# A transformer kernel whose first MLP matmul goes from groups of four to groups of six column blocks

## The chip, the core and the metric

The kernel runs on one core of a Trainium2 chip. The metric is the device time of one execution in microseconds (us). Before the change the median of 8 runs is 940.08 us (937.43 to 942.26).

The engines are PE (TensorE: matmuls), PEld (its weight loads), ACT (ScalarE: exp and gelu, which also empties the PSUM banks of scores and of the first MLP matmul), DVE (VectorE: LayerNorm, copies out of PSUM, residuals), POOL (GpSimd: masks, powers, bias) and SP, whose queue issues nearly all DMAs. PSUM, into which PE writes, has eight banks of 512 fp32 columns.

## What is computed

Two layers, the same weights in both, over x of 2048 tokens by 576. Each layer is sliding-window attention (32 heads of 18, window 256, causal) and an MLP of width 4608, both behind a LayerNorm and added to x. The MLP's input goes through LayerNorm twice, which the kernel does in one step:

```python
x = x + _A_ref(_layernorm(x, axis=-1), A_wqkv, A_wo)    # softmax attention, then @ wo
x = x + _B_ref(_layernorm(x, axis=-1), B_w1, B_b1, B_w2, B_b2)

def _B_ref(x, w1, b1, w2, b2):
    y = _layernorm(x, axis=-1)
    h = _gelu(jnp.einsum("bsd,df->bsf", y, w1) + b1)
    return jnp.einsum("bsf,fd->bsd", h, w2) + b2
```

## The kernel before

**Chunks.** The tokens are cut into chunks of 512 (four tiles of 128); two layers make eight chunks, k = 0 to 7. For each chunk the kernel projects q, k and v (`qkv`, matmul at L674), computes scores (`scores`, L744), exp on ACT (L753), masks on POOL (L774), the product with v (`pv`, L791), then in `tail` the output projection (L674 again, with `wo_sb`), the residual (L825), the LayerNorm and a DMA transpose into `xnTm`.

**MLP.** It goes in two halves of 18 column blocks of 128 (of 36). `G_part(k, hf)` makes a half of the first matmul: h = gelu(xn @ w1 + b1), transposed, 512 tokens wide, one PSUM bank a block. `mm2(k, hf)` multiplies it by w2 (L912) into banks 4, 5 and 6: for each of four tiles and two column halves three runs of six matmuls.

**A group in `G_part`.** The 576 rows of w1 are four full slabs of 128 and a remainder of 64. A group of up to four column blocks starts with `rest` (L872): one matmul of 64 rows for each block, in pairs that sit in the upper and the lower half of the array (`tile_position`), which opens the blocks' banks. Then come four full-array matmuls a block (L884) and, for each block, a gelu on ACT (L887). `rest` is one step of the plan: it takes the banks of all its blocks before its first matmul. Groups don't cross a multiple of four, so that a half of 18 goes 4, 4, 4, 4, 2 or 2, 4, 4, 4, 4. Banks come from `MM1`, 0 to 6; bank 7 belongs to `pv`; scores take two pairs out of banks 0 to 5 for each task; projections and `mm2` use 4 to 6.

**w1.** It is not kept on chip: every chunk loads it anew, by `w1_load`, in nine pieces of 512 columns into `NB1 = 4` slots of `w1_sb`. A piece is three DMAs on SP: one of 512 KB for the four slabs and two of 32 KB for the remainder. A slot's next load is asked for when its last block is through. Three pieces are asked for during chunk 0's attention ("aq3", "aq5", "aq7": when the third, fifth and seventh head group is through, counted from 0) and one when the first tile of `xnTm` has landed.

**What sets the order.** Nothing is written in execution order. `add` records steps with an engine, a cost, a latency and a priority; `Plan.schedule` lists them: at each step it takes the one that can start first by its own costs, and among those the lowest priority number, and gives it PSUM banks. `PL.nudge` shifts the priority of a stage (names such as "ea2", first half of chunk 2's scores; "gb1", second half of chunk 1's first matmul; "ma1", `mm2` of the first half; "q3.0", projection of a tile; "t3", `tail`). Scores and `G_part` keep one order among themselves (`fifo="pa"`). A step marked `hold` (`rest`) goes ahead of other PE work that would start up to 0.3 us before it. Each engine then runs its list in order and waits on semaphores where an operand or a bank is not ready.

The diff touches the constants and the table of `build_kernel` (from L409), `w1_load` (L642), `G_part` (L848), `mm2` (L898) and the first loads in the loop over chunks (L994 to L1031).

Of the kernel before, what the change touches and what calls it, by code (L numbers as in the profile page):

```python
# [6 lines left out]
BF16 = mybir.dt.bfloat16  # L7
ACT = mybir.ActivationFunctionType
ALU = mybir.AluOpType
P = 128  # L10
# [398 lines left out]
def build_kernel(nc, A_x, A_wqkv, A_wo, B_x, B_w1, B_b1, B_w2, B_b2, out):  # L409
# [8 lines left out]
    NF = F // P  # L418
    NFH = NF // 2
# [4 lines left out]
    KS = 6  # L424
    VS = 10
    PS = 3
    NB1 = 4
    NXN = 4
    NQN = 6
    WB = 6  # L430
# [8 lines left out]
    add = PL.add  # L439


    PL.nudge = {"le0+": 14.98, "q1.0": -6.62, "q1.1": 0.41, "q1.3": 0.01, "ln2": 3.13, "t0": 4.51, "ga0": -13.62, "eb1": -1.75, "q2.0": 0.19,
                "gb0": 2.91, "ln3": -4.64, "ea2": -5.93, "ma1": 3.04, "q3.0": -15.52, "q3.1": -5.81, "q3.3": -1.41, "t2": -3.4, "gb1": -2.88,
                "gb1+": -3.15, "ea3": -21.36, "mb1": -13.4, "ga2": -20.18, "ma2": 38.73, "q4.1": 1.36, "q4.2": -3.02, "q4.3": -7.11, "t3": 1.4,
                "gb2": -13.15, "gb2+": 8.35, "ln5": 1.81, "ea4": -8.49, "mb2": 6.23, "eb4": 15.12, "ma3": 29.41, "q5.0": 25.69, "q5.3": 6.9,
                "t4": 2.63, "mb3": 0.61, "eb5": 3.2, "ma4": 22.07, "ma4+": -0.97, "q6.0": 10.19, "q6.1": 9.59, "q6.3": -1.52, "t5": 0.86,
                "gb4": -2.59, "ma5": -0.01, "q7.0": -0.08, "q7.3": 14.52, "t6": 19.58, "gb5": -10.21, "mb5": 35.03, "ga6": -2.82, "ma6": 11.09,
                "t7": 1.59}

    def sb(name, shape, dtype):  # L450
        return nc.alloc_sbuf_tensor(name, shape, dtype)

    x_res = sb("x_res", [P, NT, D], FP32)
    w1_sb = sb("w1_sb", [P, NB1, 2304], BF16)
    w2_sb = sb("w2_sb", [P, NFH, D], BF16)
    wqkv = sb("wqkv", [P, KD, 3 * D], BF16)
    wo_sb = sb("wo_sb", [P, KD, D], BF16)
# [42 lines left out]
    def mm_cost(n):  # L500
        return max(n / 2400.0, 0.026) + (0.003 if n > 64 else 0.0)
# [23 lines left out]
    def dma(q, out_, in_, reads=(), writes=(), cls="w", ring=8, **kw):  # L525
        n = 2 if cls != "xr" else 4
        for s in out_.shape:
            n *= s
        kw.setdefault("lat", 2.0)
        kw.setdefault("move", n / 330e3)  # L530
        kw.setdefault("desc", n // 1152)
        add(q, lambda e: e.dma_start(out_, in_), reads=reads, writes=writes, dma=cls, ring=ring, **kw)
# [101 lines left out]

    w1n = [0]

    def straddles(group):


        return group * 4 < NFH < group * 4 + 4  # L640

    def w1_load(prio, reads=()):  # L642
        B = w1n[0]
        if B >= NK * 9:
            return
        w1n[0] += 1
        sl = B % NB1
        bb = B % 9
        cols = slice(bb * 512, (bb + 1) * 512)
        dma("sp", w1_sb[:, sl, 0:2048].rearrange("p (c f) -> p c f", c=4), B_w1[0:512, cols].rearrange("(c p) f -> p c f", p=P),  # L650
            reads=reads, writes=[f"w1a{sl}"], cls="w1", cost=0.55, lat=2.0, move=1.45, desc=512, prio=prio)
        src = B_w1[512:576, cols].rearrange("p (a b f) -> p b a f", a=2, b=2)
        if not straddles(bb):
            src = B_w1[512:576, cols].rearrange("p (b a f) -> p b a f", a=2, b=2)
        for b in range(2):
            dma("sp", w1_sb[64 * b:64 * b + 64, sl, 2048:2304].rearrange("p (a f) -> p a f", a=2), src[:, b],
                writes=[f"w1b{sl}_{b}"], cls="w1", cost=0.6, lat=1.4, move=0.22 if straddles(bb) else 0.18, desc=128 if straddles(bb) else 64, prio=prio)

    def w2_load(hf, prio, gate=False):
        for b in range(NFH // WB):  # L660
# [187 lines left out]
    def G_part(k, hf, prio):  # L848
        l, t0, nt = CH[k]
        n = nt * 128  # L850
        table("gelu", prio)
        TXm = [f"xm{k % 2}_{i}" for i in range(nt)]
        f1 = (hf + 1) * NFH
        f = hf * NFH
        while f < f1:
            n4 = min(4 - f % 4, f1 - f)
            fs = range(f, f + n4)
            f += n4
            sl = (k * 9 + fs[0] // 4) % NB1
            bks = [Bank(MM1) for _ in fs]  # L860
            rd = [f"w1a{sl}", f"w1b{sl}_0", f"w1b{sl}_1"] + TXm

            def rest(e, fs=fs, sl=sl, bks=bks):

                ins = None
                at = [(ff % 4, bk) for ff, bk in zip(fs, bks)]
                if not straddles(fs[0] // 4):
                    at = [at[i] for i in (0, 2, 1, 3)]
                for n2, (i, bk) in enumerate(at):
                    b = n2 % 2  # L870
                    col = 2048 + (i // 2 if straddles(fs[0] // 4) else i % 2) * 128
                    ins = e.matmul(bank(bk)[:, 0:n], w1_sb[64 * b:64 * b + 64, sl, col:col + 128], xnTm[64 * b:64 * b + 64, k % 2, 4, 0:n],  # L872
                                   start=True, stop=False, tile_position=(64 * b, 0))
                return ins
            add("pe", rest, reads=rd, writes=bks, cost=mm_cost(n) * (n4 // 2) + 0.21, hold=True, prio=prio, alloc=bks, fifo="pa",
                after=[f"h{ff - hf * NFH}" for ff in fs])
            for ff, bk in zip(fs, bks):
                fl = ff - hf * NFH

                def fn(e, ff=ff, sl=sl, bk=bk):  # L880
                    ins = None
                    for c in range(4):
                        col = c * 512 + (ff % 4) * 128
                        ins = e.matmul(bank(bk)[:, 0:n], w1_sb[:, sl, col:col + 128], xnTm[:, k % 2, c, 0:n], start=False, stop=(c == 3))  # L884
                    return ins
                add("pe", fn, reads=rd, writes=[bk], cost=mm_cost(n) * 4, prio=prio, lat=0.22, fifo="pa")
                add("act", lambda e, ff=ff, fl=fl, bk=bk: e.activation(hT[:, fl, 0:n], bank(bk)[:, 0:n], ACT.Gelu_apprx_tanh,  # L887
                                                                      bias=b1col[:, ff:ff + 1]),
                    reads=[bk, "b1"], writes=[f"h{fl}"] + (xin_under(fl) if k == 0 and hf == 0 else []), cost=0.145 + n * 0.00087, lat=0.17, fifo="act", prio=prio)
            if fs[-1] % 4 == 3:  # L890
                w1_load(prio - 2)
            if hf == 0 and fs[0] // 4 < nt:
                t = t0 + fs[0] // 4
                add("pool", lambda e, t=t: e.tensor_tensor(x_res[:, t, :], x_res[:, t, :], b2bc[:, :], ALU.add),  # L894
                    reads=["b2", f"h{fs[0]}"], writes=X(t), cost=1.4, prio=prio)
        table("exp", prio)

    def mm2(k, hf, prio):  # L898
        l, t0, nt = CH[k]
        for i in range(nt):  # L900
            t = t0 + i
            fin = hf == 1 and l == NL - 1
            if fin:
                osl = xn_ctr[0] % NXN
                xn_ctr[0] += 1
            for hh in range(2):
                b = Bank(FILL)
                for f0 in range(0, NFH, 6):
                    def fn(e, hh=hh, b=b, f0=f0, i=i):
                        ins = None  # L910
                        for fl in range(f0, f0 + 6):
                            ins = e.matmul(bank(b)[:, 0:HB], hT[:, fl, i * 128:(i + 1) * 128], w2_sb[:, fl, hh * HB:(hh + 1) * HB],  # L912
                                           start=(fl == 0), stop=(fl == NFH - 1))
                        return ins
                    add("pe", fn, reads=[f"h{fl}" for fl in range(f0, f0 + 6)] + [f"w2s{f0 // WB}"], writes=[b],
                        cost=6 * mm_cost(HB), lat=0.22, prio=prio + 0.05 * i, alloc=((b,) if f0 == 0 else ()))
                resid(t, hh, b, prio, outp=(osl if fin else None))
            if fin:
                dma("sp", out_dram[t * P:(t + 1) * P, :], xn[:, osl, 0:D], reads=[f"xn{osl}", f"xd{osl}"], cls="o", ring=4, cost=0.5,
                    prio=prio)  # L920
            elif hf == 1:
                ln_stats(t, prio)
# [57 lines left out]
    for k in range(NK + 1):  # L980
# [23 lines left out]
        if not last:  # L1004
            PL.stage = f"eb{k}"
            E(k, range(CUT.get(k, 4), 8), b + 1.5)
            PL.stage = f"le{k}"
            if k == 0:
                w1_load(-1, ["aq5"])
                w1_load(-1, ["aq7"])  # L1010
            if k == 1:
                for n, kk in enumerate(later):
                    x_load(CH[kk][1], CH[kk][2], [], b + 2)
                    if kk > 2:
                        stats0(kk)
# [72 lines left out]
```

## Time and profile before

| | |
|---|---|
| median of 8 runs | 940.08 us |
| the profiled execution | 940.01 us |
| its span, first to last instruction | 937.9 us |
| granted PE clock, mean of the span | 0.996 |
| first MLP matmul, full array (L884) | 1152 matmuls, 263.8 us busy |
| its remainder, `rest` (L872) | 288 matmuls, 45.0 us busy |
| second MLP matmul (L912) | 2304 matmuls, 314.8 us busy |
| projections (L674) | 1280 matmuls, 179.6 us busy |
| exp (L753) and gelu (L887) on ACT | 348.7 and 196.8 us busy |
| w1 to landing (512 KB; 32 KB) | 4.4 us; 4.1 us (medians) |
| w2 to landing (864 KB) | 6.5 us |

A profile is one execution. In it a line such as `782.13 3.63 PE L884 MATMUL ... x16` gives the start and the length of a run of equal instructions, both in us, then engine, line, operation, tiles and number; a bracket at the end gives the idle time before it and who ended it. Matmuls overlap in the pipeline, so a run ends after the next one has started; the time from start to start is what a run costs PE.

### The profile page before, as it was taken

The page shows a single profiled execution, that of the slowest core. Times are in us where ns is not written, and L with a number is a line of the kernel's source. Part 1 is how long each engine was busy: PE and PEld are TensorE (multiplying, and loading weights), DVE is VectorE, ACT ScalarE, POOL GpSimd, SP SyncE. Part 2 cuts the span into 40 slices and gives each one's busy share as a digit, 9 for nine tenths or more (in the row PEclk, how much of TensorE's full clock was granted, in tenths as well). Part 3 has the DMA queues.
Part 4 walks back from the last instruction along what each step waited for, and adds up shares of the span by engine and source line. Part 5 has one row for each costly group of instructions (what it writes and reads, how often), then busy time and mean ns, then how long its engine had stood idle before and what let it go on. Part 6 is the DMA issues. An engine that isn't in the chain of part 4 may idle for free. (4 is left out here: it accounts for less than half of the span.)

```text
span 937.9 us, 22541 instructions
## 1 busy us (share of the span) xinstructions
PE 906.8 (97%) x9382; PEld 559.9 (60%) x9382; DVE 317.1 (34%) x796; ACT 593.7 (63%) x717; POOL 373.1 (40%) x507
## 2 busy tenths in 40 slices
PE   8888999999999999999999999999999999999998
PEld 6555465664755747566564647656464674656556
DVE  6646311571225512164222614234111630223001
ACT  3777677656764777565666766657777377871541
POOL 3757444354522635143340743316452263601100
PEclk9989999999999999999999999999999999999999
DMA  9996838736089340984549360693608716094440
GB/s 217 166 203 105 193 101 227 166 58 214 2 162 239 122 109 3 221 178 79 175 75 253 67 190 26 110 257 75 194 25 226 146 48 210 13 260 118 147 139 26
DMA packets 230932, 130.06 MB, mean 139 GB/s; under 512 B 140848, under 2 KB 228656, under 8 KB 230832
## 3 DMA queue, kind: packets, MB, share of 16 engines
q1 hardware_dynamic: 221520, 120.95, 53.9%
q0 software_dynamic: 6880, 5.03, 3.3%
q10 hardware_dynamic: 2432, 2.65, 0.9%
q8 instruction: 74, 1.21, 0.6%
q14 instruction: 26, 0.21, 0.1%
HBM read 91.87 MB, written 2.36 MB: 100 GB/s over the span
## 5 line engine op out<-in xcount | busy, mean ns | idle before, releaser
L753 ACT ACTIVATE pT<-ps 128x1024 bf16<-128x1024 f32 (+2 forms) x384 | 348.7, 972 | 145.7 <-PE ps L744 144.1
L774 POOL TENSOR_SCALAR_AFFINE_SELECT pT<-pT 128x512 bf16<-128x512 bf16 (+1 forms) x368 | 281.8, 789 | 269.1 <-ACT pT L753 258.1
L912 PE MATMUL ps<-w_sb,hT 128*128 128x288 bf16 x2304 | 314.8, 286 | 1.9 <-DMA w_sb<-in_B_w_dram 1.1
L887 ACT ACTIVATE hT<-ps,b1col 128x512 bf16<-128x512 f32 x288 | 196.8, 687 | 165.4 <-PE ps L884 165.2
L884 PE MATMUL ps<-xnTm,w_sb 128*128 128x512 bf16 x1152 | 263.8, 380 | 0.0
L912 PEld LDWEIGHTS ps<-w_sb,hT 128*128 128x128 bf16 x2304 | 211.6, 97 | 74.0 <-issue 18.0
L884 PEld LDWEIGHTS ps<-xnTm,w_sb 128*128 128x128 bf16 x1152 | 106.0, 98 | 142.3 <-issue 26.9
L825 DVE TENSOR_TENSOR x_res<-ps,x_res 128x288 f32<-128x288 f32 x160 | 71.0, 449 | 252.1 <-PE ps L912 205.4
L674 PE MATMUL ps<-wqkv,xnTa 128*128 128x288 bf16 x960 | 135.4, 289 | 7.8 <-DVE qn L709 3.2
L674 PEld LDWEIGHTS ps<-wqkv,xnTa 128*128 128x128 bf16 x960 | 87.7, 98 | 41.8 <-DVE qn L709 7.0
L791 PEld LDWEIGHTS ps<-vA,pT 128*128 128x128 bf16 x2880 | 94.4, 96 | 27.4 <-POOL pT L774 9.2
L791 PE MATMUL ps<-vA,pT 128*128 128x20 bf16 x2880 | 100.3, 172 | 4.5 <-DVE attq L806 2.7
L894 POOL TENSOR_TENSOR x_res<-x_res,b2bc 128x576 f32<-128x576 f32 x32 | 44.8, 1400 | 89.4 <-ACT hT L887 89.4
L709 DVE CAST qn<-ps 128x288 bf16<-128x288 f32 x120 | 54.1, 455 | 68.2 <-PE ps L674 53.0
L744 PE MATMUL ps<-qT,kT 32*128 32x384 bf16 (+2 forms) x1216 | 64.5, 278 | 6.5 <-ACT pT L753 1.9
L599 POOL TENSOR_SCALAR vtmp<-mv_all 128x1 f32<-128x1 f32 (+1 forms) x43 | 9.0, 210 | 138.3 <-DVE mv_all L590 136.8
L801 DVE RECIPROCAL rinv<-ps 128x16 f32<-128x16 f32 x64 | 16.3, 254 | 115.4 <-PE ps L791 114.9
L696 DVE CAST vA<-ps 128x288 bf16<-128x288 f32 x64 | 28.9, 456 | 77.6 <-PE ps L674 77.5
L588 DVE BATCH_NORM_STATS2 st_all<-x_res 128x6 f32<-128x288 f32 x104 | 44.8, 447 | 9.6 <-DMA x_res<-in_A_x_dram 8.5
L872 PE MATMUL ps<-xnTm,w_sb 64*128 64x512 bf16 x288 | 45.0, 381 | 1.9 <-DMA xnTm<-xn 1.1
L674 PE MATMUL ps<-wo_sb,attT 128*128 128x288 bf16 x320 | 44.2, 286 | 2.0 <-DVE x_res L825 1.1
L611 DVE TENSOR_SCALAR xn<-x_res,mv_all,rstd 128x576 bf16<-128x576 f32 x52 | 35.8, 688 | 21.4 <-DMA xnTm<-xn 16.4
(39 smaller groups left out, 268.9 us busy)
## 6 DMA issues: line engine op xcount, KB each, us to landing
w_sb<-in_B_w_dram SPq DMA_DIRECT2D x48, 864.0 KB, 6.5
w_sb<-in_B_w_dram SPq DMA_DIRECT2D x72, 512.0 KB, 4.4
w_sb<-in_B_w_dram SPq DMA_DIRECT2D x144, 32.0 KB, 4.1
x_res<-in_A_x_dram POOLq DMA_DIRECT2D x4, 1152.0 KB, 10.0
out_dram<-xn SPq DMA_DIRECT2D x16, 144.0 KB, 1.9
wqkv<-in_A_wqkv_dram ACTq DMA_DIRECT2D x3, 576.0 KB, 7.1
hT<-in_A_x_dram SPq DMA_DIRECT2D x2, 576.0 KB, 5.9
wo_sb<-in_A_wo_dram ACTq DMA_DIRECT2D x1, 576.0 KB, 6.6
```

The costliest lines, as they stand in the source:

```text
L588: add("dve", lambda e, i=i, s=s: e.bn_stats(st_all[:, t, i, :], s[:, t, i * HB:(i + 1) * HB]), reads=res, writes=[f"st{t}_{i}"], cost=0.37 ...
L674: ins = e.matmul(bank(bs[o])[:, 0:HB], lhs(c), rhs(c, o * HB), start=(c == 0), stop=(c == KD - 1))
L709: add("dve", lambda e, b=bs[o], dst=dst: e.tensor_copy(dst, bank(b)[:, 0:HB].rearrange("p (h d) -> p h d", d=DH)), reads=[bs[o]], writes=[ ...
L744: ins = e.matmul(two(bs[j // 2])[:, j % 2, col:col + nq * 128], k_of(T0 + so)[0][32 * j:32 * j + 32, g, :], qs[32 * j:32 * j + 32, g, qo * ...
L753: add("act", lambda e, h2=h2: e.activation(pT[:, sl, 2 * h2:2 * h2 + 2, lo:hi], two(bs[h2])[:, :, lo:hi], ACT.Exp, scale=SCALE), reads=[bs ...
L774: add("pool", lambda e, ap=ap, pat=pat, sgn=sgn, kind=kind: e.affine_select(ap, ap, pattern=pat, compare_op=(ALU.is_ge if kind == "d" else ...
L791: ins = e.matmul(bank(B_O)[:, o:o + VW], pT[:, sl, j, col + qi * 128:col + (qi + 1) * 128], vA[:, (T0 + so) % VS, 4 * g + j, :], start=(fi ...
L825: add("dve", lambda e: e.tensor_tensor(x_res[:, t, sl], bank(b)[:, 0:HB], x_res[:, t, sl], ALU.add), reads=[b], writes=[f"x{t}h{hh}"], cos ...
L872: ins = e.matmul(bank(bk)[:, 0:n], w1_sb[64 * b:64 * b + 64, sl, col:col + 128], xnTm[64 * b:64 * b + 64, k % 2, 4, 0:n], start=True, stop ...
L884: ins = e.matmul(bank(bk)[:, 0:n], w1_sb[:, sl, col:col + 128], xnTm[:, k % 2, c, 0:n], start=False, stop=(c == 3))
L887: add("act", lambda e, ff=ff, fl=fl, bk=bk: e.activation(hT[:, fl, 0:n], bank(bk)[:, 0:n], ACT.Gelu_apprx_tanh, bias=b1col[:, ff:ff + 1]), ...
L912: ins = e.matmul(bank(b)[:, 0:HB], hT[:, fl, i * 128:(i + 1) * 128], w2_sb[:, fl, hh * HB:(hh + 1) * HB], start=(fl == 0), stop=(fl == NFH ...
```

## The change

`G_part` now takes a half in three groups of six blocks, and w1 comes in six pieces of 768 columns a chunk, one a group, into three slots (18 DMAs a chunk instead of 27, 768 KB and twice 48 KB a piece; the bytes are the same in total). Two pieces are asked for during chunk 0's attention ("aq3", "aq6") and the third with the first tile of `xnTm`. The step that adds b2 to x stays with every fourth block. In `mm2` the first run of six of every output but a half's first one now waits for all 18 blocks of h. The table of priorities is another one; the shifts that it holds are not repeated here.

```diff
-    NB1 = 4
+    NB1 = 3
+    GS = 6
+    GW = GS * 128
+    NGR = NF // GS
+    PAT = (6, 6, 6)
...
-    PL.nudge = {"le0+": 14.98, "q1.0": -6.62, "q1.1": 0.41, "q1.3": 0.01, "ln2": 3.13, "t0": 4.51, "ga0": -13.62, "eb1": -1.75, "q2.0": 0.19,
...
+    PL.nudge = {"ea0": -16.73, "q1.0": -5.72, "q1.1": -31.53, "q1.3": 1.29, "t0": 1.55, "ea1": -1.2, "eb1": 1.29, "ma0": 1.68, "q2.0": 33.42,
...
-    w1_sb = sb("w1_sb", [P, NB1, 2304], BF16)
+    w1_sb = sb("w1_sb", [P, NB1, 4 * GW + GW // 2], BF16)
...
-        dma("sp", w1_sb[:, sl, 0:2048].rearrange("p (c f) -> p c f", c=4), B_w1[0:512, cols].rearrange("(c p) f -> p c f", p=P),
-            reads=reads, writes=[f"w1a{sl}"], cls="w1", cost=0.55, lat=2.0, move=1.45, desc=512, prio=prio)
+        dma("sp", w1_sb[:, sl, 0:4 * GW].rearrange("p (c f) -> p c f", c=4), B_w1[0:512, cols].rearrange("(c p) f -> p c f", p=P),
+            reads=reads, writes=[f"w1a{sl}"], cls="w1", cost=0.55, lat=2.0, move=2.15, desc=512, prio=prio)
...
-        while f < f1:
-            n4 = min(4 - f % 4, f1 - f)
+        for n4 in PAT:
             fs = range(f, f + n4)
             f += n4
-            sl = (k * 9 + fs[0] // 4) % NB1
+            sls = [(k * NGR + ff // GS) % NB1 for ff in fs]
             bks = [Bank(MM1) for _ in fs]
...
-            if fs[-1] % 4 == 3:
-                w1_load(prio - 2)
...
+                if ff % GS == GS - 1:
+                    w1_load(prio - 2)
...
-                    add("pe", fn, reads=[f"h{fl}" for fl in range(f0, f0 + 6)] + [f"w2s{f0 // WB}"], writes=[b],
+                    add("pe", fn, reads=[f"h{fl}" for fl in range(f0, f0 + 6 if f0 or i + hh == 0 else NFH)] + [f"w2s{f0 // WB}"], writes=[b],
...
-                w1_load(-1, ["aq5"])
-                w1_load(-1, ["aq7"])
+                w1_load(-1, ["aq6"])
```

## The prediction

> **What bounds the kernel now.** I read the engine table first, then the stretches, then the waits of TensorE (PE), then the timeline around the changed code.
>
> Of the page:
>
> ```profile
> span 937.9 us, 22541 instructions
> PE 906.8 (97%) x9382; PEld 559.9 (60%) x9382; DVE 317.1 (34%) x796; ACT 593.7 (63%) x717; POOL 373.1 (40%) x507
> ```
>
> PE is busy 906.8 of 937.9 us; 31.1 us are left. Busy time by stretches (columns: stretch, length, busy time of PE, PEld, DVE, ACT, POOL, then granted clock, DMA):
>
> ```profile
> 0.00:50.00 50.00, 42.97 (x481) 29.91 (x482) 32.02 (x89) 27.88 (x41) 28.16 (x51) 1.00 1.26 200
> 50.00:100.00 50.00, 42.00 (x631) 27.54 (x629) 26.90 (x68) 35.61 (x44) 33.80 (x50) 0.93 0.80 149
> 300.00:450.00 150.00, 149.45 (x1612) 93.13 (x1605) 54.70 (x139) 99.82 (x120) 64.62 (x85) 1.00 0.53 123
> ```
>
> Half of what is left, 15.0 us, lies in the first 100 us, before any MLP. Later PE is all but full (149.45 of 150). So a saving must come out of PE's own time, and any new wait is paid in full. Who made PE wait, in total:
>
> ```profile
> PE ps L744 <- ACT pT L753: 3.4, 11, 0.5
> PE ps L674 <- DVE qn L709: 3.2, 7, 0.9
> PE ps L674 <- DMA xnTa<-xn: 3.1, 1, 3.1
> ...
> PE ps L912 <- DMA w_sb<-in_B_w_dram: 1.1, 1, 1.1
> ```
>
> Weights made PE wait once, 1.1 us; no wait is above 3.4 us. The changed place, PE alone:
>
> ```profile
> 782.13 3.63 PE L884 MATMUL ps<-xnTm,w_sb 128*128 128x512 bf16 x16
> 785.69 0.60 PE L872 MATMUL ps<-xnTm,w_sb 64*128 64x512 bf16 x4
> 786.23 3.63 PE L884 MATMUL ps<-xnTm,w_sb 128*128 128x512 bf16 x16
> ```
>
> Matmuls overlap, so I count from start to start. Sixteen full-array matmuls take 785.69 - 782.13 = 3.56 us. They start 0.216 us apart (the median in the trace), which makes 3.46; the last one before `rest` (L872) takes 0.312, that is 0.096 more. The four of `rest` take 786.23 - 785.69 = 0.54: pairs that run side by side, the first pair 0.22, the last pair 0.308, that is 0.085 more. So each change from full array to row-tiled matmuls and back costs 0.096 + 0.085 = 0.18 us. Scores (L744, 32 rows) show the same: the matmul before them takes 0.218 instead of 0.122.
>
> **What the change removes.** `rest` runs 6 instead of 10 times a chunk, 48 instead of 80 times in all, with the same 288 matmuls. In the built order of PE's instructions the changes from full array to row-tiled fall from 269 to 239, and as many back (30 and not 32, since a few groups stood beside scores). **-30 x 0.18 = -5.4 us.** PE is nearly full where these lie, so I take them whole.
>
> [...] Here six banks of seven are wanted at once instead of four, and the next three terms price that from rows.
>
> **New wait 1: a group right behind a group.** Group n+1 needs six banks; one is free, five must come from group n, so the gelu of its fifth block must be done. The fifth block stands before the sixth, so PE does 4 x 0.216 + 0.096 = 0.96 us between. What is needed is seen once in before, where a group happened to want the bank of the last block but one:
>
> ```profile
> 395.85 3.63 PE L884 MATMUL ps<-xnTm,w_sb 128*128 128x512 bf16 x16
> ...
> 398.65 0.69 ACT L887 ACTIVATE hT<-ps,b1col 128x512 bf16<-128x512 f32 x1 [0.18 <-PE ps L884]
> ...
> 399.48 0.61 PE L872 MATMUL ps<-xnTm,w_sb 64*128 64x512 bf16 x4
> ```
>
> The gelu ends at 399.34, `rest` starts 0.14 later, and the sixteen took 3.63 instead of 3.56: 0.07 us of wait. In the changed order 25 of the 48 groups stand like this: **+25 x 0.07 = +1.8 us.** The other groups have a projection's or a second MLP matmul's bank as their last one, which VectorE empties in 0.46 us; such reuses at 0.73 to 0.81 us mostly cost nothing in before. Bounds: 0 (the gelu has a head start) and 48 x 0.2 = 9.6, 0.2 being what `rest` at 170.43 paid at a distance of 0.83.
>
> **New wait 2: a group right behind scores.** A score task owns four banks until its two exps are done. A group of four finds banks beside them; six of seven banks leave out one, so `rest` must outwait the last exp. Before:
>
> ```profile
> 211.00 0.40 PE L744 MATMUL ps<-qT,kT 32*128 32x256 bf16 x8
> ...
> 211.45 1.94 ACT L753 ACTIVATE pT<-ps 128x1024 bf16<-128x1024 f32 x2 [0.35 <-PE ps L744]
> ...
> 212.90 0.61 PE L872 MATMUL ps<-xnTm,w_sb 64*128 64x512 bf16 x4
> ...
> 213.40 1.28 ACT L928 ACT_TABLE_LOAD   x1
> ```
>
> `rest` ran at 212.90, before the exps ended at 213.39, 2.39 us after the score started. Twelve of the fourteen halves that follow scores show the same 2.39; the two of chunk 4's scores, a smaller task, end 1.4 after it. So `rest` would now need 2.46, or 1.5. With each matmul of the changed order at the start-to-start time of its kind in before, the distance from the last score's start to `rest` is, in order, 2.63, 3.01, 2.26, 4.48, 3.22, 2.89, (chunk 4: 2.20, 2.37), 2.26, 3.22, 2.21, 2.63, 2.26 and 0.81 us. What is missing sums to **+2.5 us**, two thirds of it in the last one. Before paid 0.8 for such waits (0.2 at 329.34, 0.57 at 661.2), which go: -0.8. Bounds: 1.6 (small stalls on the way cover the short ones) and 6 (ACT 0.4 late in all). Queued behind a late `rest` is all of PE; ACT uses the pause for its table load (1.28), which then no longer delays the first gelu.
>
> **New wait 3: one bank for the filler.** Inside a group of six one bank is left. The changed order weaves projections between blocks (a projection right before a first MLP matmul 39 times, before 2). Where one takes the bank of the one before it, a block of 0.86 us lies between; 28 reuses at 0.8 to 0.9 us, before 6. DVE needs 0.15 to start, 0.46 for the copy and some 0.05 for the signal, 0.66: 0.2 to spare. DVE is busy 34% of the time, mostly in pieces of 0.45; one in the way for over 0.2 us is met about 0.34 x 0.25 / 0.45 = 0.19 of the time, costing 0.13 on average: 28 x 0.19 x 0.13 = **+0.7 us.** Bounds: 0, and 28 x (0.69 - 0.2) = 14 if the longest DVE piece (0.69, L611) were always ahead.
>
> **What the new priorities move.** (a) The first score of the last chunk idles 1.43 us before 740.31, since its third query tile is projected only 5.6 us of PE work earlier; now 21.5 us: -1.5. Chunk 6 goes the other way, from 52 to 6.8 us, its second score task from 15.8 to 5.0. By the 7.1 us that chunk 7 needed (5.6 + 1.5) this costs 0.3 to 2.1; I take 0.7. Net **-0.8**. (b) In the last attention stretch (second half of the last chunk's scores, ahead of the second MLP half of chunk 6) ACT needs 12 x 2.06 (two exps of 1.02 each) + two table loads of 1.28 + 0.9 for the gelu left over = 28.2 us, against 27.9 of PE work; now 28.9 of PE work. **-0.3.** (c) The first 1,100 PE instructions are nearly the same. Ten projection matmuls (1.2 us) that filled the wait for the first `rest` at 104 us (0.6 left) now come after it; against that, the first output projection follows the attention after 4.3 us of PE work, not 6.9, so the LayerNorm chain that feeds `rest` starts earlier. The transposes take 3.4 us to land, so 4.3 is barely enough. I take 0, with -2 to +1.2.
>
> **At nothing.** Loads of w1: three slots of six blocks, each slot used once a half, its refill due 26 us of PE work later, against 4.4 us (512 KB) to 6.5 us (864 KB) to landing. If that cover were gone, a group would wait some 6 us. 72 fewer loads, 24 of them large, free SP some 79 us (nine took 9.77 at 781.70), but all of PE's DMA waits are 7.3 us; a larger load ahead of a transposed tile can also delay it. I take 0, bounds -2 and +2.
> [...]
> The second MLP matmul now wants all 18 blocks before every output but the first; that first one is 2.2 us of PE work, over the 0.9 us that the last gelu takes.
>
> **Sum.** -5.4 + 1.8 + 2.5 - 0.8 + 0.7 - 0.8 - 0.3 = -2.3 us. The profiled execution took 940.01, the median of the runs is 940.08, so the two scales agree: **937.7**.
>
> **Rivals.**
> 1. *The waits are hidden.* The gelus are ahead, small stalls cover the exps, the copies are in time: 0, 1.6 and 0 for the three new waits, -5.7 in all: 934.3. For it: ACT has more room in its tightest stretch, and a stall of before that comes next shrinks when an earlier one grows. Against: the row at 399.48. Chance 0.22.
> 2. *Nothing in the end.* Chunk 6 pays 2.1 and the start 1.2: -2.3 + 1.4 + 1.2 = +0.3, 940.3. For it: these distances (5.0, 4.3) are at the edge. Chance 0.2.
> 3. *Slower: the single bank.* If DVE has other work ahead in half of the 28 reuses, at some 0.35 us each, wait 3 is 4.9 and not 0.7: +1.9, 941.9. It decides from 3.0 us on, 0.11 a reuse. For it: LayerNorm and residuals run on DVE in the same stretches, and one projection of before waited 0.66 at a distance of 0.94. Against: most at 0.8 and above cost nothing. Chance 0.16.
> That the change doesn't take hold can't be: the built order has 48 groups and 18 loads a chunk.
>
> **Numbers.** Forecast 937.7 with 0.42 (936 to 939.5). About 0.2% (1.9 us) is what a measurement can tell from no change. Faster (below 938.2): rival 1 and three quarters of the forecast, 0.54. Same: the rest of the forecast and most of rival 2, 0.28. Slower: rival 3 and a tail of rival 2, 0.18. The range, 933 to 942, leaves out the tails beyond rivals 1 and 3.
>
> **What would show it.** Right: the first MLP matmul in runs of 24 with a `rest` of six between, 0.76 us each; 0.07 us before it in the pure stretches; a pause of PE behind the last score, ended by an exp, largest (1.65 us) before the second MLP half of chunk 6, right behind the last chunk's scores; no idle before the last chunk's first score. Wrong: PE's idle time after 100 us above 20 us, waits of `rest` (L863 there) on exps above 5 us, projections (L670 there) waiting on DVE's copies above 7 us (3.2 now), or DMA waits on w1.

## Result and profile after the change

The changed kernel takes 933.45 us (median of 11 runs, 932.18 to 935.92; a twelfth took 938.36 and is not in it) against 940.55 (32 runs, 936.93 to 944.73) for the kernel before: ratio 0.9927, 95% interval 0.9912 to 0.9941. The forecast was 937.7: the direction was right and the size too small, 2.3 us instead of 7. The time lies less than half a microsecond inside the lower end of the forecast's range (933 to 942). The profiled execution took 933.05 us. Of its page, span and engine table, then the groups of the first MLP matmul's remainder (`rest`, L863 here) and of the second MLP matmul, and the loads of w1:

```profile
span 931.3 us, 22417 instructions
PE 901.5 (97%) x9382; PEld 565.9 (61%) x9382; DVE 319.8 (34%) x796; ACT 594.0 (64%) x717; POOL 371.8 (40%) x507
...
L863 PE MATMUL ps<-xnTm,w_sb 64*128 64x512 bf16 x288 | 39.5, 378 | 2.7 <-ACT pT L749 2.2
...
L904 PE MATMUL ps<-w_sb,hT 128*128 128x288 bf16 x2304 | 314.9, 286 | 1.2 <-DVE x_res L821 1.0
...
w_sb<-in_B_w_dram SPq DMA_DIRECT2D x48, 768.0 KB, 5.0
```

The instructions of PE are the same in number; `rest` is busy 39.5 us instead of 45.0, since its matmuls now run in longer rows (six in 0.82 us, four in 0.61). The three stretches of the prediction (length, busy time of PE, PEld, DVE, ACT, POOL, clock, DMA):

```profile
0.00:50.00 50.00, 41.94 (x468) 29.46 (x472) 31.71 (x88) 26.28 (x39) 27.59 (x50) 1.00 1.32 185
50.00:100.00 50.00, 44.10 (x680) 29.16 (x672) 28.89 (x75) 39.84 (x47) 35.92 (x53) 1.00 0.95 173
300.00:450.00 150.00, 148.76 (x1553) 93.53 (x1553) 52.89 (x134) 95.50 (x117) 60.63 (x79) 1.00 0.50 127
```

From 50 to 100 us PE does 680 matmuls instead of 631 and the clock is 1.00 instead of 0.93; later it is as full as before, a little less so. Who makes PE wait, over the whole span (total us, times, longest):

```profile
PE ps L740 <- ACT pT L749: 4.9, 15, 1.1
PE ps L670 <- DVE qn L705: 4.2, 6, 1.6
PE ps L670 <- DVE x_res L821: 3.1, 3, 1.9
...
PE ps L863 <- ACT pT L749: 2.2, 3, 1.9
...
PE ps L670 <- DMA xnTa<-xn: 0.5, 1, 0.5
```

The 3.1 us for a transposed tile (`xnTa`) have shrunk to 0.5, no line for a wait on weights is left, and a new one is there: `rest` waits 2.2 us for exps. PE in the changed place:

```profile
862.25 0.82 PE L863 MATMUL ps<-xnTm,w_sb 64*128 64x512 bf16 x6
863.00 5.35 PE L875 MATMUL ps<-xnTm,w_sb 128*128 128x512 bf16 x24
868.36 0.82 PE L863 MATMUL ps<-xnTm,w_sb 64*128 64x512 bf16 x6
```

From `rest` to `rest` 868.36 - 862.25 = 6.11 us: 0.75 for six of `rest`, 5.36 for the 24 that follow. Without a wait those would take 24 x 0.216 + 0.096 = 5.28; the rest, 0.08 us, is the new wait 1.

To sum this up over the kernel, I gave every matmul its median start-to-start time in before, by its kind and its neighbours. The sum of these is the **floor**: what PE needs in the built order if it never waits and the clock is full. What the span has above it is the **excess**, that is, waits, half clock and the end behind PE's last matmul; it is split at the first `rest`, where the first chunk's MLP begins. Each kernel twice; single runs of before have spans 9 us apart, so differences below 1 or 2 us mean nothing here.

| profile | span | floor | first `rest` at | excess up to it | excess after it |
|---|---|---|---|---|---|
| before | 937.9 | 890.3 | 104.1 | 22.9 | 20.0 |
| before, again (e10) | 940.2 | 890.3 | 106.7 | 25.6 | 19.6 |
| after | 931.3 | 884.4 | 99.3 | 18.8 | 23.4 |
| after, again (e11) | 933.5 | 884.4 | 101.1 | 20.6 | 23.7 |

In the means the change gives -5.9 (floor) - 4.55 (start) + 3.75 (later) = -6.7 us. So the switches paid what was forecast, and what comes behind the first `rest` took most of it back, as forecast (+3.1); what the forecast had at 0 is the start.

### The profile page after: what moved, and what is told of

The parts are those of the page before. It is cut to its first block, busy times and chain, and to the rows that moved or that the text cites. A ratio compares the mean times of both kernels' runs of the same rounds, so it can differ in the third digit from the quotient of the medians.

```text
span 931.3 us, 22417 instructions
## 1 busy us (share of the span) xinstructions
PE 901.5 (97%) x9382; PEld 565.9 (61%) x9382; DVE 319.8 (34%) x796; ACT 594.0 (64%) x717; POOL 371.8 (40%) x507
## 5 line engine op out<-in xcount | busy, mean ns | idle before, releaser
L875 PEld LDWEIGHTS ps<-xnTm,w_sb 128*128 128x128 bf16 x1152 | 109.4, 98 | 133.8 <-issue 17.4
L863 PE MATMUL ps<-xnTm,w_sb 64*128 64x512 bf16 x288 | 39.5, 378 | 2.7 <-ACT pT L749 2.2
L740 PEld LDWEIGHTS ps<-qT,kT 32*128 32x128 bf16 x1216 | 19.5, 92 | 33.6 <-issue 19.2
```

The lines of the kernel that those rows point to most:

```text
L740: ins = e.matmul(two(bs[j // 2])[:, j % 2, col:col + nq * 128], k_of(T0 + so)[0][32 * j:32 * j + 32, g, :], qs[32 * j:32 * j + 32, g, qo * ...
```

## Experiments

Theory A, after the result: fewer switches save 5.9 us, waits behind exps and gelus cost some 4, and the other 4.5 come from the order of the first 100 us, where PE no longer waits for a transposed tile. The rival B: the start is scatter or belongs to the profile, and the groups alone make the gain. The ratios are to the kernel before on the same chip.

**e1: the groups with the old priorities.**

```diff
-    PL.nudge = {"ea0": -16.73, "q1.0": -5.72, "q1.1": -31.53, ...
+    PL.nudge = {"le0+": 14.98, "q1.0": -6.62, "q1.1": 0.41, ...
```

> Groups of six and the six loads of the changed kernel, with the priorities of before. Theory A (the switches pay 5.4 us, the bank waits of six banks eat most of it, and the gain of the first 100 us is the work of the new priorities): PE's order up to the first `rest` is that of before, so the wait of 3.1 us for a transposed tile near 50 us and the half clock after it stay, and the first `rest` starts near 104 us. Then -5.4 for 30 switches, +2.0 for 28 groups close behind a group, +3 to +5 for scores close before a group (two at the distance that cost 1.96 in the changed kernel, four that cost 0.24): 939 to 942. Theory B (groups and loads do it all, the start too, since fewer w1 loads stand in the queue before the transposes): 933 to 935, first `rest` near 99 us.

961.89 us, ratio 1.0231 (1.0200 to 1.0263): both theories missed the total, by 20 us and more. The floor is 884.6, so the switches were saved as in after; but the excess behind the first `rest` is 51.9 us. Its waits of PE:

```profile
PE ps L671 <- DMA xnTa<-xn: 11.3, 4, 6.1
PE ps L741 <- ACT pT L750: 7.5, 21, 1.1
```

With the longer groups under the old priorities a transposed tile comes 6.1 us late, exps make scores wait 21 times, and the granted clock is 0.984 in the mean of the span, which is 31 us at half. For the start alone, theory A held: the first `rest` stands at 105.6, with a wait of 3.3 us for `xnTa`, as in before.

**e2: the new priorities with the old groups.**

```diff
-    PL.nudge = {"le0+": 14.98, "q1.0": -6.62, "q1.1": 0.41, ...
+    PL.nudge = {"ea0": -16.73, "q1.0": -5.72, "q1.1": -31.53, ...
```

> Groups of four, nine loads a chunk and four slots as before, with the priorities of the changed kernel. Theory A: the first `rest` starts near 100 us instead of 104 (-3.6 after the 1.2 us of projections that are put off), no half clock near 50 us; the switches stay (266), so that the time is 935 to 938. Theory B: the start is as before, 940 to 942.

973.90 us, ratio 1.0353 (1.0323 to 1.0383): here too both theories missed the total, by over 30 us. The first `rest` comes at 97.3, earlier than in any other run, and the wait for `xnTa` near 53 us is gone, so the new start order carries over (21 of the matmuls that after runs ahead of its first `rest` come behind it here); the excess behind it is 60.2 us. The heaviest wait, and a stretch of it:

```profile
PE ps L743 <- ACT pT L752: 13.3, 28, 1.1
```

```profile
830.00:860.00 30.00, 22.93 (x359) 12.43 (x358) 4.49 (x12) 23.71 (x27) 16.72 (x22) 0.66 0.33 110
```

ACT is busy 23.71 of 30 us, PE starves behind its exps, and the granted clock is 0.66: half clock for 20.5 us of these. So "what the groups give" and "what the priorities give" are no two separate terms: each without the other costs 21 to 34 us. How these divide into waits and half clock was not taken apart further.

**e3: the price of a switch.** The last pair of each `rest` is moved in front of the fifth block's matmuls: the same matmuls, 48 more switches there and back.

```diff
-                for ff, sl, bk in zip(fs, sls, bks):
+                for ff, sl, bk in list(zip(fs, sls, bks))[0:4]:
...
+                late = [(x, y, z) for x, y, z in zip(fs, sls, bks)][4:6] if ff == fs[4] else []
...
+                    for f2, s2, k2 in late:
...
+                        e.matmul(bank(k2)[:, 0:n], w1_sb[64 * b:64 * b + 64, s2, col:col + 128], ...)
```

> The changed kernel, with the last pair of each `rest` put right before the fifth block's matmuls; same matmuls, banks, plan and loads, but 48 more changes from full array to row-tiled and back. If a switch costs 0.18 us wherever PE is full: +8.7 us, 942 (the first pair group is shorter, so ACT starts 0.2 us earlier, worth nothing). If switches are hidden by PE's waits, below +4: under 937.

944.57 us, ratio 1.005 (1.003 to 1.0069): 11.1 us above after, 8.7 expected. PE:

```profile
875.38 0.61 PE L863 MATMUL ps<-xnTm,w_sb 64*128 64x512 bf16 x4
875.92 3.63 PE L882 MATMUL ps<-xnTm,w_sb 128*128 128x512 bf16 x16
879.49 0.39 PE L878 MATMUL ps<-xnTm,w_sb 64*128 64x512 bf16 x2
879.81 1.90 PE L882 MATMUL ps<-xnTm,w_sb 128*128 128x512 bf16 x8
881.71 0.61 PE L863 MATMUL ps<-xnTm,w_sb 64*128 64x512 bf16 x4
```

A group takes 881.71 - 875.38 = 6.33 us instead of 6.11, so a switch there and back costs 0.22; 48 x 0.22 = 10.6. The term of 0.18 that the forecast built on is right, if anything low.

**e4: `rest` waits pair by pair.** Each pair of `rest` waits for its own two banks instead of all six. The order is the same.

```diff
+            elif t.hold:
+                for j in range(len(t.writes) // 2):
+                    self.S.add(t.eng, lambda e, t=t, j=j: t.fn(e, j), names(t.reads), names(t.writes[2 * j:2 * j + 2]), ...)
...
-                for ff, sl, bk in zip(fs, sls, bks):
+                for ff, sl, bk in list(zip(fs, sls, bks))[2 * j:2 * j + 2]:
```

> The changed kernel with the same order on every engine, but each pair of `rest` waits for its own two banks only, instead of the first pair for all six. Theory A: the 25 waits of 0.07 us go (-1.8), the three of 0.06 to 0.24 behind scores go (-0.5), and the one of 1.96 us shrinks by the 0.44 us of two pairs, and if the half clock behind it goes too, another -1.7: 929.5 to 931.5. Rival: what the waits cost is taken up by later waits anyway, 933 to 934.

931.35 us, ratio 0.9906 (0.9881 to 0.9931), 2.1 us below after by the medians; the intervals of the two ratios overlap. PE of e4:

```profile
860.10 5.35 PE L878 MATMUL ps<-xnTm,w_sb 128*128 128x512 bf16 x24
865.38 0.82 PE L866 MATMUL ps<-xnTm,w_sb 64*128 64x512 bf16 x6
```

865.38 - 860.10 = 5.28, exactly what 24 matmuls and one switch need: wait 1 is gone, and with it its price of 0.07 to 0.08 a group is confirmed. The waits of `rest` on exps fall from 2.2 to 1.0 us, the later excess from 23.4 to 19.4. The half clock behind the last exps stays (3.4 us from 811.4; the clock is 0.92 from 800 to 822 us).

**e5: the new start alone.** Before, with the six priorities of the first stages from after.

```diff
-    PL.nudge = {"le0+": 14.98, "q1.0": -6.62, "q1.1": 0.41, "q1.3": 0.01, "ln2": 3.13, "t0": 4.51, "ga0": -13.62, ...
+    PL.nudge = {'ga0': -13.62, 'eb1': -1.75, 'q2.0': 0.19, ... 'ea0': -16.73, 'q1.0': -5.72, 'q1.1': -31.53, 'q1.3': 1.29, 't0': 1.55, 'ea1': -1.2}
```

> The kernel of before (groups of four, nine loads) with the changed priorities of the first stages alone: chunk 0's and the first half of chunk 1's scores, chunk 1's projections, the second LayerNorm stage, chunk 0's tail and the first loads. From the second chunk's MLP on PE's order is that of before. Theory (half of the gain is made before the first `rest`, by priorities and not by groups): the first `rest` near 98 us instead of 104, 1.6 us of it projections put off, no half clock near 50 us: 935.5 to 938. Rival (the start differs by chance from run to run, or the gain is given back later): 939 to 941.

940.81 us, ratio 1.0014 (0.9995 to 1.0033): nothing gained, theory A missed. The first `rest` does come earlier (101.9 against 104.1 and 106.7), 1.6 us of it by projections put off, but of the wait for `xnTa` 1.8 us stay. The six shifts are not the whole new start: `q2.0`, the projection of chunk 2's first tile, keeps its 0.19 here and has 33.42 in after. In the built orders PE does as in after only up to this wait. There after projects the second tile of chunk 2, and e5 the first, whose transpose was issued at 48.48 and took 6.1 us to land (PE, then SP, of e5):

```profile
54.63 0.79 PE L668 MATMUL ps<-wqkv,xnTa 128*128 128x288 bf16 x5 [1.80 <-DMA xnTa<-xn]
```

```profile
48.48 1.20 SPq L625 DMA_TRANSPOSE xnTa<-xn  x1
```

Its excess is 22.4 before and 21.7 behind the first `rest`, where the order of the last 6590 matmuls is that of before: it stands inside before's scatter.

**e6: work in the longest wait.** In after, 17 dummy matmuls fill the pause ahead of the `rest` at 813.20 (their results are not used).

```diff
+            if t.hold and t.stage == "gb6" and not filled:
+                filled.append(t)
+                bk = t.writes[0]
+                self.S.add("pe", lambda e: self.warm_fn(e, bk.no, 17), ["warm"], [f"pb{bk.no}"])
```

> The changed kernel with 17 idle-filling matmuls (1.9 us, their result is overwritten) where PE waits 1.9 us for the last exps, before the second MLP half of chunk 6. If the half clock of 3.4 us behind that wait comes from the wait, it goes and the time falls by 1.4 to 1.7: 931.5 to 932. If the clock falls anyway, 933 to 934.

932.96 us, ratio 0.9937 (0.9920 to 0.9954). The reason for trying it is this stretch of PE in after:

```profile
808.84 0.40 PE L740 MATMUL ps<-qT,kT 32*128 32x384 bf16 x8
810.37 0.40 PE L740 MATMUL ps<-qT,kT 32*128 32x256 bf16 x8 [1.13 <-ACT pT L749]
...
813.20 0.82 PE L863 MATMUL ps<-xnTm,w_sb 64*128 64x512 bf16 x6 [1.89 <-ACT pT L749]
813.96 0.58 PE L787 MATMUL ps<-vA,pT 128*128 128x20 bf16 x16
814.39 1.87 PE L875 MATMUL ps<-xnTm,w_sb 128*128 128x512 bf16 x4
```

The four matmuls behind the wait take 1.87 us; at full clock they take about half (0.22 each, as in 5.35 for 24 above). With the dummies in the pause, in e6:

```profile
811.53 2.02 PE L583 MATMUL ps<-warm 128*128 128x256 bf16 x17
813.57 0.82 PE L868 MATMUL ps<-xnTm,w_sb 64*128 64x512 bf16 x6
```

The stretch of 22 us around it, first after, then e6 (the clock is the last column but two):

```profile
800.00:822.00 22.00, 18.97 (x238) 11.40 (x235) 3.45 (x9) 15.67 (x18) 9.50 (x13) 0.92 0.49 144
```

```profile
800.00:822.00 22.00, 20.77 (x261) 13.23 (x260) 3.45 (x9) 16.27 (x19) 9.87 (x14) 1.00 0.49 145
```

With the pause filled the clock stays at 1.00; in after it is 0.50 from 814.20 to 817.60. So the wait costs a second time: 3.4 us at half clock behind it. The six profiles in which this pause is not filled have half clock: 3.4 us here in after, after again and e4 (0.92 from 800 to 822 us in each), 6.8 us in e3 (0.97 from 750 to 850), and in e8 and e9 some 7 us behind their first 100 us, an estimate from the means of their spans (0.994 and 0.996) and of those 100 us (0.985 and 1.00). The two in which it is filled (e6, e7) have none here (1.00 from 800 to 822). In time e6 gains 0.5 us by the medians and nothing by the ratios (0.9937 against 0.9927), which the scatter covers; the profiles show the granted clock at 1.00 instead of 0.92, the clock on the wall does not prove what that is worth.

**e7: e4 and e6 together.** The two edits above in one kernel.

> Both: `rest` waits pair by pair, and the 17 matmuls fill the wait. If the two gains add: 929.5 to 930.5. If the half clock stays: 931 to 932.

929.47 us (927.8 to 932.23), ratio 0.9904 (0.9883 to 0.9924): 4.0 us below after by the medians. By its ratio it can't be told from e4 (0.9906), so that the two gains add is not shown. The later excess is 16.7, with the 2.0 us of filler counted as work.

**e8: the loads of w1 in halves.** Each load of 768 KB becomes two of 384 KB, 24 loads a chunk instead of 18; the order of PE is the same.

```diff
-        dma("sp", w1_sb[:, sl, 0:4 * GW]...
+        for hh in range(2):
+            part = slice(bb * GW + hh * 384, bb * GW + hh * 384 + 384)
+            dma("sp", w1_sb[:, sl, 0:4 * GW].rearrange("p (c f) -> p c f", c=4)[:, :, hh * 384:hh * 384 + 384], ...
```

> The changed kernel with each large load of w1 as two of 384 KB (24 loads a chunk instead of 18), the same order on PE. Theory (loads are hidden behind two groups and more): 933 to 934. Rival (each load costs queue time that someone waits for): 48 more loads, +1 us or more.

932.93 us, ratio 0.9944 (0.9923 to 0.9965): no difference from after that the scatter doesn't cover. The number of loads is off the path, as forecast: 48 more of them cost nothing that these runs can tell.

**e9: the first tail as late as before.** In after, one start priority is put back.

```diff
-    PL.nudge = {"ea0": -16.73, "q1.0": -5.72, "q1.1": -31.53, "q1.3": 1.29, "t0": 1.55, ...
+    PL.nudge = {'ea0': -16.73, 'q1.0': -5.72, 'q1.1': -31.53, 'q1.3': 1.29, ... 't7': -1.96, 't0': 4.51}
```

> The changed kernel with the priority of chunk 0's tail (output projection, LayerNorm, transposes) of before: 4.51 for 1.55. PE's order differs only between its 961st and 1138th matmul, just ahead of the first `rest`; all after it is as in the changed kernel. Theory (part of the gain is that the tail starts earlier in the start, where PE waits for chains): the first `rest` comes 1 to 2.5 us later than the 99.3 to 101.7 of the runs with the new start, and the time is 1 to 2 us longer, 934.5 to 935.5. Rival: nothing, 933 to 934.

933.25 us (12 runs), ratio 0.9947 (0.9927 to 0.9966), first `rest` at 99.1: no effect. The place of the first `tail` is not what made the start faster.

**e10 and e11: both kernels again,** unchanged, for the scatter of the start.

> The kernel of before once more, for a second profile: what of the difference between the two profiles is the kernel's and what is the single execution's. If the start is really later in before, the first `rest` is near 104 to 105.5 us again, and the half clock is met in the first 100 us again; the time is 940.

> The changed kernel once more, for a second profile: first `rest` at 99 to 102 us, 25 waits of 0.07 us again, the wait of 1.9 us near 811 us and the half clock behind it again; the time is 933 to 934.

940.68 and 934.49 us (ratios 1.0007, 0.9987 to 1.0027, and 0.9948, 0.9928 to 0.9968). The first `rest` comes later in before than in after in both pairs (104.1 and 106.7 against 99.3 and 101.1). PE in before, then in before again, for the same two runs of five projection matmuls:

```profile
49.74 0.79 PE L674 MATMUL ps<-wqkv,xnTa 128*128 128x288 bf16 x5
53.62 1.38 PE L674 MATMUL ps<-wqkv,xnTa 128*128 128x288 bf16 x5 [3.09 <-DMA xnTa<-xn]
```

```profile
50.41 0.79 PE L674 MATMUL ps<-wqkv,xnTa 128*128 128x288 bf16 x5
54.10 1.38 PE L674 MATMUL ps<-wqkv,xnTa 128*128 128x288 bf16 x5 [2.90 <-DMA xnTa<-xn]
```

and in after:

```profile
51.63 0.79 PE L670 MATMUL ps<-wqkv,xnTa 128*128 128x288 bf16 x5
52.91 0.77 PE L670 MATMUL ps<-wqkv,xnTa 128*128 128x288 bf16 x5 [0.49 <-ACT pT L749]
```

Behind the wait of some 3 us five matmuls take 1.38 instead of 0.79 us: half clock again, for 6.8 us (the clock is 0.87 from 36 to 62 us in both, and 1.00 in after). The queue of SP says why after doesn't wait here. In before these matmuls read the first tile of chunk 2, whose transpose is issued at 47.06 and takes 6.5 us to land; in after they read the second tile of chunk 2, whose transpose is issued at 43.22 and takes 2.6 us. The first tile's transpose follows there at 47.76 and takes 7.6 us. First before, then after:

```profile
47.06 1.23 SPq L631 DMA_TRANSPOSE xnTa<-xn  x1
```

```profile
43.22 1.23 SPq L634 DMA_TRANSPOSE xnTa<-xn  x1
...
47.76 1.48 SPq L634 DMA_TRANSPOSE xnTa<-xn  x1
```

Half clock itself is not gone from the new start: after has none in its first 100 us (the clock is 1.00), after again has 6.8 us, in two pieces behind other waits (at 44.9 and 82.5; 0.93 from 36 to 62 us, 0.96 from 62 to 100).

## Why the prediction was right, and where its sum was off

The time is nearer to rival 1's 934.3 than to the forecast's 937.7, but not by rival 1's mechanism: the waits that it took as hidden were paid (2.0 and 2.5 us). What is missing is the start, term (c). That the terms behind the first `rest` come so near (+3.1 forecast, +3.75 measured) is in part luck: some costs that nobody had priced stand against some that were not paid.

**Switches, -5.4: right.** The floor, which holds nothing but the order, falls by 5.9; e3 prices one switch there and back at 0.22 us against 0.18.

**New wait 1, +1.8: right.** 25 groups pay 0.07 to 0.08 us each (one 0.27), 2.0 us in all; e4 takes the wait away, and 24 matmuls are back at 5.28.

**New wait 2, +2.5: right, and one cost behind it was missed.** From start to start, and less the 0.08 us that a change to row-tiled matmuls costs there, `rest` behind scores is late at 201.6, 537.9, 764.5 and 813.2 us: 0.24 + 0.24 + 0.06 + 1.96 = 2.5 us, the last one where the forecast had put 1.65. ACT shows the last exp, and the table load that uses the pause:

```profile
809.29 3.77 ACT L749 ACTIVATE pT<-ps 128x1024 bf16<-128x1024 f32 x4 [0.35 <-PE ps L740]
813.08 1.28 ACT L920 ACT_TABLE_LOAD   x1
```

Missed was the half clock behind it: 3.4 us in after, from 814.2 (clock 0.50), and gone in e6 and e7 (1.00), where the pause is filled. The matmuls in it take twice as long (four in 1.87 us, against 0.22 each), so in after it costs at most 1.7 us. e6's later excess and its filler together, 19.7 + 2.0, are 1.7 below after's 23.4, which agrees.

**New wait 3, +0.7, and rival 3, the single bank: not seen.** Projections wait on DVE's copies 4.2 us (it was 3.2), but all of it in the first 100 us; behind that it falls from 0.7 to 0. One other wait of 1.85 us appeared near 517, of an output projection for a residual on DVE, which itself stood 2.07 us behind a DMA; no row of before pointed to it.

**(a), -0.8, and (b), -0.3.** The last chunk's first score has no idle time ahead of it any more, so the 1.5 are right; the 0.7 for chunk 6 were not paid. The 0.3 of (b) are not seen: ACT still makes PE wait at the end of this stretch, 1.13 us at 810.37 in after (shown with e6), more than in before:

```profile
812.47 0.40 PE L744 MATMUL ps<-qT,kT 32*128 32x256 bf16 x8 [0.29 <-ACT pT L753]
```

Before's wait of 1.1 us for a weight is gone, which the forecast didn't count; the new ones at 517 and 810 us took its place.

**Loads of w1, 0: right** (e8).

**The step that failed is (c): the first 1,100 PE instructions "are nearly the same", taken as 0 with bounds of -2 and +1.2.** Measured are -4.1 (18.8 against 22.9) and -5.0 (20.6 against 25.6). The two orders differ in the kind of the matmul from the 323rd on, and earlier than that in the tile that a projection reads. The forecast compared them by the distance of the first output projection and by ten projections that move behind the first `rest`; it followed neither the tiles nor the queue of SP. The largest single wait of before, 3.1 us for `xnTa`, stood in the lines that the prediction itself showed, and was taken as given (the 3.4 us that it names as the longest is a total of eleven waits). The clock row of before, 0.93 from 50 to 100 us, was shown and passed over too.

`xnTa` has one place for each of a chunk's four tiles. In after two shifts of priority act together. The second tile of chunk 1 is projected early (`q1.1` went from 0.41 to -31.53), which frees the second place, so that the second tile of chunk 2 is transposed at 43.22. And the first tile of chunk 2 is put off (`q2.0` went from 0.19 to 33.42), so that PE projects the second one, which has landed. Three profiles with the old start order (before, again, e1) wait 2.9 to 3.3 us for the first tile, with 3.4 to 6.8 us at half clock (0.87, 0.87 and 0.93 from 36 to 62 us); nine with the new one (after, again, e2, e3, e4, e6 to e9) don't wait for a tile there. e5, with the first shift and not the second, waits 1.8. Of the rest of the gain, 1.1 us (1.5 in e10) is a wait of the first `rest` for a transposed tile of `xnTm`, which is gone in after and in after again. Half clock in the first 100 us is less on the whole, 6.8 to 10.2 us in the three with the old order and 0 to 6.8 in the nine (mean clock 0.95 to 0.97, and 0.97 to 1.00), but single runs overlap.

**What stays open.** e1 and e2 tie the start to the table of priorities and not to the groups: with the old table the groups of six start as before does (3.3 us of wait, first `rest` at 105.6), with the new one the groups of four start as after does (none, 97.3). These are one profile each, and both kernels lose over 20 us later, so no run shows the 4 us of the start in the time by themselves; e5, the try at that, left out one of the shifts. That the two shifts do it is read from the built orders and the traces; no run changed `q1.1` or `q2.0` alone. Of the start priorities only the tail's was tried by itself (e9: not that one).

## What to carry to other kernels

Count the switches between full-array and row-tiled matmuls in the built order and price them by a gap to the next matmul: that sum held to half a microsecond. A group that takes more banks at one wait pays where it follows another group closely (25 of 48 here, 0.07 to 0.08 us each); let each pair wait for its own banks (e4, -2.1 us by the medians). Look up every wait of the old profile above 1 us and ask whether the new order moves what it waits for, along the DMA queue as well. Compare two orders by the tiles that the instructions read, and not only by their kinds: the order that looked "nearly the same" freed a place, and so issued a transfer, 4 us earlier, and then used another tile first.

## What the runs showed of the hardware

A wait of PE of 1.89 us in after (up to 813.20), with one of 1.13 us shortly ahead of it (up to 810.37), was followed by 3.4 us at half clock: the granted clock is 0.50 from 814.20 to 817.60 us. In after again the same two waits were followed by 3.4 us too (0.92 from 800 to 822 us); in e3, where the longest waits for exps are 1.9 and 1.1 us as well, it was 6.8 us (0.97 from 750 to 850). With the pause filled (e6, e7) the clock stayed at 1.00 there. Waits of 2.9 to 3.3 us near 53 us came with 6.8, 6.8 and 3.4 us at half clock (before, again, e1: 0.87, 0.87 and 0.93 from 36 to 62 us); in before the clock is 0.50 already from 52.90 us on, while the wait ends at 53.62. It is not the same each time: a wait of 1.6 to 1.7 us near 43.5 us, which ten profiles share, came with half clock in five of them (after again, e3, e5, e6, e7: 0.93 from 36 to 62 us) and without it in the other five (after, e2, e4, e8, e9: 1.00). So the measurement decides: in after, with PE busy 97% of the span, the 1.89 us had up to 1.7 us more behind them.
